# Fixed items of an expert layer: tokens found by products on TensorE in place of a scatter and a read-back through memory

## The chip, the cores and the metric

The kernel runs on one NeuronCore of a Trainium2 chip. The metric is the device time of one execution in microseconds (us). PE is TensorE (products and transposes), with PEld its weight loads; DVE is VectorE, ACT ScalarE, POOL GpSimd, SP SyncE. Matrices of weights and tokens lie in HBM, working tiles in SBUF, results of PE in PSUM.

## The reference

Three layers in a row, in fp32. (1) Attention over 2 batches, 8 heads, 576 places of 64 numbers, with rotated q and k. (2) A dense layer on the 1152 tokens: `g = h * sigmoid(1.702 h)` of `h = x @ w_in`, then `g @ w_out`, 512 to 2048 to 512. (3) A layer of eight experts, of which each token uses one:

```python
logits = x @ w_gate                      # (1152, 8)
expert_idx = np.argmax(logits, axis=1)
gate_w = softmax(logits)[token, expert_idx]
for i in range(N):                       # in order of tokens
    e = expert_idx[i]
    if counts[e] < capacity:             # 288
        disp[e, counts[e]] = x[i]; pos[i] = counts[e]; counts[e] += 1; keep[i] = True
h = np.maximum(einsum('ecd,edf->ecf', disp, w1), 0.0)
y = einsum('ecf,efd->ecd', h, w2)
out[i] = gate_w[i] * y[expert_idx[i], pos[i]]   # rows that are not kept stay 0
```

## The kernel before, in words

**Attention** (`Attention`, to L650) goes through 8 pairs of heads; an explicit table of times sets the order of its instructions. It writes its result transposed and split into a high and a low part (`xt`), because products are made of three parts each: high by high, high by low, low by high.

**The dense layer** (`Experts.first`, L904) takes the tokens in three cuts, 0 to 511, 512 to 767 and 768 to 1151. Each cut runs over the 16 slices f of the 2048 hidden numbers (`ffn`, L859): slice f of the weights is cut into high and low (`halves`, L829, `hl`: ACT copies, DVE subtracts), PE makes the hidden products `h` (L853), ACT and DVE apply the function and cut its result into `gh` and `gl` (L893 to L895), and two slices later PE adds the products into `y` (L883). At the end of a cut `y` holds one tile of 128 tokens per bank; each is copied into `row` and sent to HBM as `x2` (L935). For the first two cuts the 8 logits of a token are eight DVE instructions per tile (L943, `dot`); for the last cut (three tiles) PE transposes the rows (L967) and multiplies them by the gate weights (L976).

**Routing** (`route`, L979) runs once per batch, when the last tile with tokens of the batch has its logits: batch 0 during the third cut, batch 1 behind it. DVE finds the expert of each token, PE counts the tokens ahead of it with products of bf16 matrices of zeros and ones (`rank`, L1020 and L1023), and DVE works out `lin`, the number of the token's slot in a list (L1045 to L1054). Then POOL scatters, tile by tile, an entry of four numbers per token (row, row in the output, gate) into the list `slots` in HBM (L1069, five instructions per batch), reads the list back per item (`gather`, L1136, `ent`), and gathers the rows of `x2` that it names (L1146, `got`).

**Items.** An item is one expert with up to 288 tokens. Four items are fixed, two per batch: 3 blocks of 96 tokens, 2 of 112, 3 of 96 and 1 of 96 (`STATIC`, L35). Before an item starts, `turn` (L1157) transposes its gathered rows on PE (`tg`, L1164) into `xt`. `second` (L1205) runs `ffn` over 8 slices of the expert's weights, transposes the result back (`tr`, L1218), scales by the gate on DVE (L1221) and scatters the rows to the output (L1193). The fourth item is made by `few` (L1224). Items 2 and 3 belong to batch 1; the transposes of item 2 stand behind the last step of item 1's loop (hook 0 at L1331). A loop for surplus items (L1334) runs only when an expert has more tokens than the fixed items hold; otherwise a branch skips it.

**What sets the order.** Each engine runs its own instructions strictly in the order in which a scheduler wrote them, and waits on semaphores for the others. The scheduler ranks instructions of the whole program, so a change in routing also moves weight cuts and products that it does not touch. The loads of the weights stand on SP's queue; SP reads an item's expert from `etab` (L1296) before it loads that item's weights.

## Time and profile before

| | |
|---|---|
| median of 3 runs | 440.02 us (439.24 to 440.18) |
| the profiled execution's own time | 437.69 us |
| its span, first to last instruction | 436.0 us |
| PE busy | 423.7 us (97%) |
| DVE, ACT, POOL busy | 326.0, 264.7, 137.2 us |
| granted clock of PE | 0.998 of 2.4 GHz |

The profile is one execution. An engine's timeline lists its instructions in order of start; neighbours of one kind are drawn together (x4), the second number is the time from the first start to the last end, and a bracket behind the row says how long the engine sat idle before it and what released it. Since PE works as a pipeline, the pitch of its products is read from the start of one row to the start of the next, not from a row's length.

### The profile page before, as it was taken

The page shows a single profiled execution, that of the slowest core. Times are in us where ns is not written, and L with a number is a line of the kernel's source. Part 1 is how long each engine was busy: PE and PEld are TensorE (multiplying, and loading weights), DVE is VectorE, ACT ScalarE, POOL GpSimd, SP SyncE. Part 2 cuts the span into 40 slices and gives each one's busy share as a digit, 9 for nine tenths or more (in the row PEclk, how much of TensorE's full clock was granted, in tenths as well). Part 3 has the DMA queues.
Part 4 walks back from the last instruction along what each step waited for, and adds up shares of the span by engine and source line. Part 5 has one row for each costly group of instructions (what it writes and reads, how often), then busy time and mean ns, then how long its engine had stood idle before and what let it go on. Part 6 is the DMA issues. An engine that isn't in the chain of part 4 may idle for free.

```text
span 436.0 us, 8504 instructions
## 1 busy us (share of the span) xinstructions
PE 423.7 (97%) x3150; PEld 349.5 (80%) x3150; DVE 326.0 (75%) x762; ACT 264.7 (61%) x556; POOL 137.2 (31%) x129
## 2 busy tenths in 40 slices
PE   7899999999999999999999999999999999999994
PEld 3566766666675888888899999898898999999992
DVE  5666766678998989997379988979546489766663
ACT  1798989988777334444456565574446356563662
POOL 1988778693347200000000000007330006531012
PEclk9999999999999999999999999999999999999999
DMA  8624413711343566665015000100824447686501
GB/s 269 234 114 153 152 47 107 250 30 50 98 161 114 194 214 213 238 234 208 2 72 208 34 3 0 50 0 1 291 76 135 154 144 181 199 273 221 213 21 53
DMA packets 20686, 58.96 MB, mean 135 GB/s; under 512 B 3542, under 2 KB 5910, under 8 KB 20641
## 3 DMA queue, kind: packets, MB, share of 16 engines
q1 hardware_dynamic: 18016, 53.98, 36.9%
q0 software_dynamic: 1664, 3.62, 2.8%
q10 hardware_dynamic: 960, 0.79, 0.5%
q8 instruction: 26, 0.43, 0.4%
q14 instruction: 20, 0.16, 0.1%
HBM read 51.79 MB, written 6.67 MB: 134 GB/s over the span
## 4 chain that ended last, share of the span: by engine, by line
PE 73%; issue 12%; DVE 4%; DMA 4%; POOL 3%; ACT 1%; SPq 0%; POOLq 0%; DVEq 0%; ACTq 0%
PE y L883 23%; PE h L853 23%; PE t L601 8%; PE s L488 7%; PE t L528 7%; PE s L477 2%; PE s L747 2%; POOL out L1193 2%; DMA turns<-in_turns 1%; DMA slots<-entry,r_at 1%; DMA wf<-in_w 1%; DVE pp L500 1%; POOL got L1146 1%; POOL slots L1069 1%; DVE hl L834 1%
## 5 line engine op out<-in xcount | busy, mean ns | idle before, releaser
L853 PE MATMUL h<-xt,hl 128*128 128x256 f32 (+4 forms) x828 | 145.7, 317 | 0.0
L853 PEld LDWEIGHTS h<-xt,hl 128*128 128x128 f32 x828 | 127.2, 189 | 9.9
L834 DVE TENSOR_TENSOR hl<-wf,hl 128x1024 fp32r<-128x1024 f32 x69 | 84.5, 1225 | 28.2 <-ACT hl L833 26.8
L833 ACT ACTIVATE hl<-wf 128x1024 fp32r<-128x1024 f32 x69 | 73.2, 1060 | 37.4 <-PE y L883 21.9
L883 PE MATMUL y<-hl,gh 128*128 128x512 f32 x288 | 82.6, 392 | 0.0
L1069 POOL DMA_INDIRECT slots<-entry,r_at x10 | 16.6, 1658 | 186.1 <-DVE r_ends L992 183.7
L883 PEld LDWEIGHTS y<-hl,gh 128*128 128x128 f32 x288 | 53.1, 188 | 9.6
L500 DVE TENSOR_SCALAR_CACHE_REDUCE pp<-s 128x576 f32<-128x576 f32 x64 | 46.0, 755 | 18.9 <-PE s L488 18.5
L893 ACT ACTIVATE g<-h 128x256 f32<-128x256 f32 (+2 forms) x45 | 21.8, 484 | 57.8 <-PE h L853 55.6
L512 ACT ACTIVATE pp<-pp,nm 128x576 f32<-128x576 f32 x64 | 49.2, 774 | 11.2 <-DVE pp L500 11.1
L461 POOL TENSOR_TENSOR qk<-qk,turns 128x640 f32<-128x640 f32 (+1 forms) x30 | 44.9, 1514 | 20.2 <-DMA qk<-in_qk 20.2
L883 PE MATMUL y<-hl,gl 128*128 128x512 f32 x144 | 49.7, 391 | 0.0
L488 PE MATMUL s<-qk 64*128 64x288 f32 x256 | 40.4, 421 | 1.3 <-DVE qk L463 0.7
L601 PE MATMUL t<-pt,vr 128*64 128x288 f32 x256 | 38.0, 417 | 0.0
L895 DVE TENSOR_TENSOR gl<-g,gh 128x512 fp32r<-128x512 f32 (+2 forms) x48 | 26.6, 559 | 13.1 <-ACT gh L894 12.6
L528 PEld LDWEIGHTS t<-ident,pp 64*128 64x128 f32 x576 | 25.8, 138 | 13.1 <-issue 4.2
L943 DVE SCALAR_TENSOR_TENSOR dot<-row,dots 128x512 f32<-128x512 f32 x48 | 32.9, 685 | 1.8 <-ACT row L931 1.4
L883 PE MATMUL y<-gh,hl 128*128 128x288 f32 (+1 forms) x192 | 33.4, 289 | 0.0
L407 ACT ACTIVATE pt<-t 128x512 f32<-128x512 f32 (+1 forms) x55 | 28.5, 542 | 6.7 <-PE t L528 6.4
L528 PE MATMUL t<-ident,pp 64*128 64x64 f32 x576 | 29.8, 228 | 1.6 <-ACT ptr L407 1.1
L883 PEld LDWEIGHTS y<-hl,gl 128*128 128x128 f32 x144 | 26.4, 188 | 4.3
L488 PEld LDWEIGHTS s<-qk 64*128 64x128 f32 x256 | 24.1, 188 | 6.1 <-DVE pp L500 1.6
(189 smaller groups left out, 583.7 us busy)
## 6 DMA issues: line engine op xcount, KB each, us to landing
wf<-in_w SPq DMA_DIRECT2D x32, 512.0 KB, 5.3
qk<-in_qk SPq DMA_DIRECT2D x14, 640.0 KB, 7.2
raw<-in_w_in SPq DMA_DIRECT2D x16, 512.0 KB, 4.4
raw<-in_w_out SPq DMA_DIRECT2D x16, 512.0 KB, 3.3
vr<-in_v SPq DMA_DIRECT2D x8, 320.0 KB, 4.9
out<-got SPq DMA_DIRECT2D x9, 256.0 KB, 3.7
dots<-in_w_dots SPq DMA_DIRECT2D x4, 512.0 KB, 4.5
x<-row SPq DMA_DIRECT2D x8, 256.0 KB, 3.4
```

Source lines behind the costliest of these rows:

```text
L407: return e.activation(out=out, in_=x, func=AF.Copy)
L461: e.tensor_tensor(out=u, in0=u, in1=self.turns[:, k, ts], op=ALU.mult)
L488: nc.tensor.matmul(both[h][:, n, 0:HALF], q[hs, at:at + P], k[hs, key:key + HALF], start=True, stop=True)
L500: self.nc.vector.tensor_scalar(out=self.room(p, i).rearrange("p (n k) -> p n k", n=2), in0=self.open.pop(("s", p, i))[:, :, 0:HALF], scala ...
L512: self.nc.scalar.activation(out=x, in_=x, func=AF.Exp, scale=-1.0, bias=self.nm[p % 2][:, i:i + 1], accum_out=self.sum[p % 2][:, i, 0:1],)
L528: self.nc.tensor.transpose(banks[b][:, at:at + 64], x[bs], self.ident[bs, bs])
L601: self.nc.tensor.matmul(o[h * 64:h * 64 + 64], x, y, start=j < 2, stop=j > 7)
L833: ins = nc.scalar.activation(out=hl[:, 0], in_=t, func=AF.Copy)
L834: self.last = nc.vector.tensor_tensor(out=hl[:, 1], in0=t, in1=hl[:, 0].bitcast(F32), op=ALU.subtract).ins
L853: ins = self.nc.tensor.matmul(h, u, v, start=m == 0, stop=m == len(ops) - 1)
L883: nc.tensor.matmul(y[j][:, 0:DM if rows else w], u, v, start=f == LAG and m == 0, stop=f == n + LAG - 1 and m == 2,)
L943: ins = nc.vector.scalar_tensor_tensor(out=self.weights.m2.tile([P, DM], F32, tag="m", name="dot"), in0=row, scalar=1.0, in1=self.dots[e], ...
```

## The change

In words: (1) `lin` is no longer only an address. `mark` compares the numbers 0 to 511 (`seats`, loaded once) with each token's slot number: five DVE instructions per batch give matrices of zeros and ones, 128 tokens by 512 (batch 0) or 384 (batch 1) seats, in bf16. (2) `find` multiplies them on PE by a table with six columns per token (two digits of its number, a constant, and the gate in three bf16 parts): `who`, five products for each block of 96 or 112 seats, so 25 for batch 0 and 20 for batch 1. DVE adds the parts up and writes the entry of each seat into `found`. (3) The row gathers read `found`. Scatter and read-back of the list remain only in the branch for surplus items. (4) `find(1)` stands in the loop of item 0, `find(0)` right behind `route(0)`. (5) Of the last cut's three tiles only two are transposed and multiplied on PE; the third gets eight `dot` instructions on DVE. (6) The gate is worked out earlier in `route`.

```diff
@@ -800,9 +808,13 @@
 
         load(self.rows, d["rows"])
         load(self.masks, d["masks"])
+        load(self.seats, d["seats"])
         before = self.three.tile([P, DM], F32, name="got", bufs=4)[:, 0:P]
         load(before, d["before"])
         nc.vector.tensor_copy(out=self.before, in_=before)
+        digits = self.three.tile([P, DM], F32, name="got", bufs=4)[:, 0:3 * B * NC]
+        load(digits, d["digits"])
+        nc.vector.tensor_copy(out=self.digits[:, :, :, 0:3], in_=digits.rearrange("p (b k c) -> p b k c", b=B, c=3))
         load(self.small, d["small"])
         load(self.gate, d["w_gate"])
         pad = self.three.tile([P, DM], F32, name="got", bufs=4)[0:TT, 0:NSLOT // TT * 4].bitcast(I32)
...
@@ -925,7 +937,7 @@
         work = []
         for n, (k, t) in enumerate(zip(range(k0 // P, k1 // P), y)):
             row = self.three.tile([P, DM], F32, name="row")
-            if last and n % 2:
+            if last and n == 1:
                 nc.vector.tensor_copy(out=row, in_=t)
             else:
                 nc.scalar.activation(out=row, in_=t, func=AF.Copy)
...
@@ -935,10 +947,8 @@
                     nc.sync.dma_start(out=self.x2[b][lo - b * S:hi - b * S, :], in_=row[lo - k * P:hi - k * P])
             work.append((row, [self.logits[b][:, k - b * (NC - 1)] for b in range(B) if 0 <= k - b * (NC - 1) < NC]))
         if last:
-            self.turned_logits(work)
-            known(k1 // P - 1)
-            return
-        for k, (row, out) in zip(range(k0 // P, k1 // P), work):
+            self.turned_logits(work[:-1])
+        for k, (row, out) in list(zip(range(k0 // P, k1 // P), work))[-1 if last else 0:]:
             for e in range(E):
                 ins = nc.vector.scalar_tensor_tensor(
                     out=self.weights.m2.tile([P, DM], F32, tag="m", name="dot"),
...
@@ -949,8 +959,9 @@
                     op1=ALU.mult,
                     accum_out=out[0][:, e:e + 1],
                 )
-                if self.placed:
-                    self.tc.add_manual_dep(ins.ins, self.placed, Weights.order, reason="order")
+                before = self.low if last else self.placed
+                if before:
+                    self.tc.add_manual_dep(ins.ins, before, Weights.order, reason="order")
             for x in out[1:]:
                 nc.vector.tensor_copy(out=x, in_=out[0])
             known(k)
...
@@ -1052,31 +1069,16 @@
         tt(lin, lin, s2, ALU.add)
-        at = new("at", NC, dt=I32)
-        placed = v.tensor_copy(out=at, in_=lin)
+        placed = self.mark(b, lin, gate)
         self.placed = placed.ins.name
...
-        done = []
-        for j in range(NC):
-            ins = nc.gpsimd.indirect_dma_start(
-                out=self.slots,
...
+        self.tokens.append((at, entry))
+        if b == 0:
+            self.find(b)
...
@@ -1133,6 +1135,85 @@
+    def mark(self, b, lin, gate):
+
+        v, digits = self.nc.vector, self.digits[:, b]
+        rest = self.one.tile([P, NC], F32, name="r_rest")
+        v.tensor_copy(out=digits[:, :, 3], in_=gate)
+        v.tensor_tensor(out=rest, in0=gate, in1=digits[:, :, 3], op=ALU.subtract)
+        v.tensor_copy(out=digits[:, :, 4], in_=rest)
+        v.tensor_tensor(out=digits[:, :, 5], in0=rest, in1=digits[:, :, 4], op=ALU.subtract)
+        n = sum(math.prod(STATIC[i]) for i in (2 * b, 2 * b + 1))
+        room = self.two.tile([P, ND, HALF], F32, name="yt", bufs=1).rearrange("p j c -> p (j c)").bitcast(BF16)
+        last = self.one.tile([P, SEATS], BF16, name="taken")
+        self.taken = []
+        for k in range(NC):
+            x = (room[:, k * SEATS:(k + 1) * SEATS] if k < NC - 1 else last)[:, 0:n]
+            ins = v.tensor_scalar(
+                out=x, in0=self.seats[:, 0:n], scalar1=lin[:, k:k + 1], scalar2=-2.0 * b * HALF,
+                op0=ALU.subtract, op1=ALU.is_equal,
+            )
+            self.taken.append(x)
+        return ins
+
+    def find(self, b):
+
+        v, digits = self.nc.vector, self.digits[:, b]
+        groups = [(2, 3)] if b else [(0,), (1,)]
+        seat, column = 0, 0
+        t = self.ps_m.tile([P, 512], F32, tag="m", name="who")
+        for items in groups:
+            size = STATIC[items[0]][1]
+            blocks = sum(STATIC[i][0] for i in items)
+            u = t[0:size, column:column + 6 * blocks].rearrange("p (i c) -> p i c", c=6)
+            for i in range(blocks):
+                for k in range(NC):
+                    x = self.taken[k][:, seat:seat + size]
+                    self.nc.tensor.matmul(u[:, i], x, digits[:, k], start=k == 0, stop=k == NC - 1)
+                seat += size
+            column += 6 * blocks
+            total = self.one.tile([P, 4, 2], F32, name=f"total{items[0]}")[0:size, 0:blocks]
+            v.tensor_reduce(out=total, in_=u.rearrange("p i (a c) -> p i a c", c=3), axis=AX.X, op=ALU.add)
+            ents = self.one.tile([P, 4, 4], I32, name=f"found{items[0]}")[0:size, 0:blocks]
+            for c, far in (0, FAR), (2, FAR + b * S):
+                v.tensor_scalar(out=ents[:, :, c], in0=total[:, :, 0], scalar1=float(far), scalar2=None, op0=ALU.add)
+            v.tensor_copy(out=ents[:, :, 3].bitcast(F32), in_=total[:, :, 1])
+            at = 0
+            for item in items:
+                ent, rows = ents[:, at:at + STATIC[item][0]], []
+                at += STATIC[item][0]
+                for i in range(ent.shape[1]):
+                    row = self.three.tile([P, DM], F32, name="got", bufs=4)[0:size]
+                    self.fetch(row, b, ent[:, i, 0:1])
+                    rows.append(row)
+                self.found[item] = ent, rows
+
...
@@ -1328,17 +1402,22 @@
                 self.clear()
 
         for i in range(3):
-            self.second(found[i][0], x[i], self.expert(i, sp), ((4, 0, 4)[i], lambda: turn(i + 1)))
+            hooks = {(4, TURN, 4)[i]: lambda: turn(i + 1)}
+            if i == 0:
+                hooks[FIND] = lambda: self.find(1)
+            self.second(found[i][0], x[i], self.expert(i, sp), hooks)
         self.few(found[3][0], x[3], self.expert(3, sp))
         n = nc.values_load(self.etab[0:1, ITEMS:ITEMS + 1], min_val=4, max_val=ITEMS)
-        with tc.If(n > 4, label="more"), tc.For_i(4, n, 1, iteration_sync="staggered") as i:
-            ent, rows = self.gather(i, [0, 1])
-            tc.stage_boundary()
-            self.cut = []
-            x = self.turn(rows, 0)
-            tc.stage_boundary()
-            self.second(ent, x, self.expert(i, sp))
-            tc.stage_boundary()
+        with tc.If(n > 4, label="more"):
+            self.scatter()
+            with tc.For_i(4, n, 1, iteration_sync="staggered") as i:
+                ent, rows = self.gather(i, [0, 1])
+                tc.stage_boundary()
+                self.cut = []
+                x = self.turn(rows, 0)
+                tc.stage_boundary()
+                self.second(ent, x, self.expert(i, sp))
+                tc.stage_boundary()
 
 
 def whole(ctx, tc, d):
```

How the change moves instructions is shown at three places. `hl0_74` and `hl1_75`, or `hl_74` and `hl_75`, are the two halves of the ring of cut weights.

PE at the end of the third cut, before and then after (`tr<-ident,row` transposes a tile, `tr<-gate` makes its logits, `h 128x288` belongs to item 0):

```order
L853 MATMUL h<-xt,hl_74 128x288 x2
L967 MATMUL tr<-ident,row 128x128 x4
L853 MATMUL h<-xt,hl_74 128x288 x22
L967 MATMUL tr<-ident,row 128x128 x8
L976 MATMUL tr<-gate,yt 128x8 x4
L883 MATMUL y_3921<-gh,hl_74 128x288 x2
L853 MATMUL h<-xt,hl_75 128x288 x12
L976 MATMUL tr<-gate,yt 128x8 x4
L976 MATMUL tr<-gate,got 128x8 x4
```

```order
L865 MATMUL h<-xt,hl_74 128x288 x2
L978 MATMUL tr<-ident,row 128x128 x4
L865 MATMUL h<-xt,hl_74 128x288 x22
L978 MATMUL tr<-ident,row 128x128 x4
L987 MATMUL tr<-gate,yt 128x8 x4
L895 MATMUL y_3941<-gh,hl_74 128x288 x2
L895 MATMUL y_3942<-gh,hl_74 128x288 x2
L895 MATMUL y_3943<-gh,hl_74 128x288 x2
L865 MATMUL h<-xt,hl_75 128x288 x12
L987 MATMUL tr<-gate,yt 128x8 x4
```

One tile's four transposes and its four products with the gate weights are gone.

DVE where the slot numbers of batch 1 become final, before and then after (`yt` and `taken` hold the matrices of `mark`):

```order
L992 TENSOR_TENSOR r_lin<-r_lin,r_s_3807 128x5
L834 TENSOR_TENSOR hl_75<-wf,hl_75 128x1024
L992 TENSOR_TENSOR r_lin<-r_lin,r_s_3808 128x5
L1056 CAST r_at<-r_lin 128x5
L992 TENSOR_TENSOR r_ends<-r_base,r_items 128x8
```

```order
L1003 TENSOR_TENSOR r_lin<-r_lin,r_s_3859 128x5
L846 TENSOR_TENSOR hl_74<-wf,hl_74 128x1024
L1003 TENSOR_TENSOR r_lin<-r_lin,r_s_3860 128x5
L1152 TENSOR_SCALAR yt<-seats,r_lin 128x384 x4
L1152 TENSOR_SCALAR taken<-seats,r_lin 128x384
L1075 CAST r_where_3880<-r_lin 128x5
L1003 TENSOR_TENSOR r_ends<-r_base,r_items 128x8
```

The five comparisons stand right behind the final slot numbers, and the cut of weights ahead of them is one slice further on (the other half of the ring).

PE where item 0 ends and item 1 (`128x224`) begins, before and then the start of the new products of batch 1:

```order
L883 MATMUL y3_3924<-gh_4134,hl1_75 128x288 x2
L883 MATMUL y3_3924<-gl_4135,hl1_75 128x288
L853 MATMUL h_4260<-xt_59,hl0_74 128x224 x12
L883 MATMUL y0_3921<-gh_4163,hl1_75 128x288 x2
L883 MATMUL y1_3922<-gh_4163,hl1_75 128x288 x2
```

```order
L895 MATMUL y3_3944<-gh_4197,hl1_75 128x288 x2
L895 MATMUL y3_3944<-gl_4198,hl1_75 128x288
L865 MATMUL h_4323<-xt_59,hl0_74 128x224 x6
L895 MATMUL y0_3941<-gh_4226,hl1_75 128x288 x2
L1172 LDWEIGHTS yt_3873
L1172 MATMUL who_4108<-digits_1876,yt_3873 96x6
L895 MATMUL y1_3942<-gh_4226,hl1_75 128x288 x2
```

Four of the first five `who` stand between products of the layers, one by one; the other sixteen follow each other.

## Rows read from the trace of the kernel before

**Rows 1.** Timeline by windows, all engines: busy us and instructions, granted clock, DMA share, GB/s.

```profile
core 0: us, PE busy (x) PEld busy (x) DVE busy (x) ACT busy (x) POOL busy (x), PEclk, DMA share, GB/s
336.00:346.00 10.00, 10.00 (x83) 9.80 (x82) 5.63 (x13) 4.81 (x9) 0.00 (x0) 1.00 0.56 204
350.00:360.00 10.00, 10.00 (x79) 10.00 (x78) 9.22 (x32) 4.91 (x8) 0.00 (x0) 1.00 0.49 157
360.00:370.00 10.00, 10.00 (x84) 10.00 (x82) 9.11 (x37) 6.56 (x12) 6.74 (x5) 1.00 0.75 172
410.00:420.00 10.00, 10.00 (x81) 10.00 (x80) 5.76 (x11) 6.56 (x15) 0.00 (x0) 1.00 0.38 144
```

**Rows 2.** Timeline of PE, last tile of tokens: start us, us, line, operation.

```profile
336.26 0.66 PE L967 MATMUL tr<-ident,row 128*128 128x128 f32 x4
336.67 3.14 PE L853 MATMUL h<-xt,hl 128*128 128x288 f32 x22
339.65 1.03 PE L967 MATMUL tr<-ident,row 128*128 128x128 f32 x8
...
344.07 1.04 PE L976 MATMUL tr<-gate,got 128*128 128x8 f32 x8
344.97 0.38 PE L883 MATMUL y<-gl,hl 128*128 128x288 f32 x1
```

**Rows 3.** Timeline of PE, rank products of batch 1 and transposes behind them.

```profile
349.53 0.20 PE L1020 MATMUL rank<-r_oh,before 128*128 128x48 bf16 x1
349.57 0.27 PE L1023 MATMUL rank<-r_oh,ones 128*128 128x40 bf16 x5
349.70 0.58 PE L1164 MATMUL tg<-ident,got 112*128 112x112 f32 x4
350.05 0.51 PE L883 MATMUL y<-gh,hl 128*128 128x288 f32 x2
```

**Rows 4.** Source lines 1020, 967, 1218, weight loads: ns min/median/max, first and last start.

```profile
L1020 PEld LDWEIGHTS <-before x2: 96/96/97, 290.2 to 349.5; 128*128 128x128 bf16 x2
...
L967 PEld LDWEIGHTS tr<-ident,row x12: 138/140/143, 336.3 to 340.3; 128*128 128x128 f32 x12
...
L1218 PEld LDWEIGHTS tr<-ident,yt x32: 124/127/134, 368.9 to 425.8; 128*96 128x96 f32 x24, 128*112 128x112 f32 x8
```

**Rows 5.** Source line 703 and groups by line, DVE (busy us, mean ns, idle before).

```profile
L703 DVE TENSOR_SCALAR m<-raw x32: 388/422/1035, 102.3 to 201.0; 128x512 uint32<-128x512 uint32 x32
...
L943 DVE SCALAR_TENSOR_TENSOR dot<-row,dots 128x512 f32<-128x512 f32 x48 | 32.9, 685 | 1.8 <-ACT row L931 1.4
...
L834 DVE TENSOR_TENSOR hl<-wf,hl 128x1024 fp32r<-128x1024 f32 x69 | 84.5, 1225 | 28.2 <-ACT hl L833 26.8 <-issue 1.0
```

**Rows 6.** Timeline of DVE, the seat number of batch 1 is final.

```profile
359.51 0.16 DVE L992 TENSOR_TENSOR r_lin<-r_lin,r_s 128x5 f32<-128x5 f32 x1
```

**Rows 7.** Timeline of PE where items read what routing found.

```profile
299.70 1.92 PE L853 MATMUL h<-xt,hl 128*128 128x384 f32 x10
...
364.75 1.49 PE L853 MATMUL h<-xt,hl 128*128 128x224 f32 x12
...
379.90 0.49 PE L1164 MATMUL tg<-ident,got 96*128 96x96 f32 x4
...
390.11 2.81 PE L853 MATMUL h<-xt,hl 128*128 128x288 f32 x20
```

**Rows 8.** Timeline of POOL, batch 1: first scatter, first row gather.

```profile
360.16 1.01 POOL L1069 DMA_INDIRECT slots<-entry,r_at  x1 [31.90 <-DVE r_ends L992]
...
375.76 1.04 POOL L1146 DMA_INDIRECT got<-x,ent  x1 [1.82 <-PE h L853]
```

**Rows 9.** Source line 1296, SP reads an item's expert: count, ns, first and last start.

```profile
L1296 SPq TENSOR_LOAD <-etab x4: 267/286/466, 303.2 to 366.1; - x4
```

**Rows 10.** Timeline of all engines, the end.

```profile
430.17 0.68 ACT L1292 ACTIVATE row<-y,ent 96x512 f32<-96x512 f32 x1 [2.17 <-PE y L1282]
431.13 0.92 POOL L1193 DMA_INDIRECT out<-row,ent  x1 [1.70 <-ACT row L1292]
```

More of the change, by code (lines that the diff above doesn't have):

```diff
@@ L36 @@
 ROWS = 20
+SEATS = 512
+FIND = 3
+TURN = 0
 NSLOT = ITEMS * HALF
@@ L775, in prepare @@
         self.oh = one.tile([P, NC + 1, E], BF16, name="r_oh")
+        self.seats = one.tile([P, SEATS], F32, name="seats")
+        self.digits = one.tile([P, B, NC, 6], BF16, name="digits")
         self.small = one.tile([P, NC * E + 2 * ROWS * E + ROWS], F32, name="small")
@@ L1209, in second @@
         w = blocks * size
-        y = self.ffn(x, [lambda f=f: self.slice_of(expert, f) for f in range(F2 // P)], self.relu, {hook[0]: hook[1]} if hook else {})
+        y = self.ffn(x, [lambda f=f: self.slice_of(expert, f) for f in range(F2 // P)], self.relu, hooks)
         yt = self.two.tile([P, ND, HALF], F32, name="yt", bufs=1)
@@ L1310, in run @@
         found, x = {}, {}
+        self.found, self.tokens = found, []
         def turn(i):
```

68 lines of the change are left out of this document (40 added, 28 removed).

## The prediction, made before the changed kernel ran

> **What bounds the kernel now.** I read the table of waits first, which names no wait of PE in the stretch of the change, and then the timeline by windows, because a busy PE can still be one that crawls. In the four windows of [rows 1] PE is busy for all of the 10 us; the reader is to see that the counts fit as well: the last window holds 81 products, 123 ns each, and 22 products of 288 columns fill the time from 336.67 to the next transposes at 339.65, some 135 ns each with the changes of kind [rows 2]. There is no hole that a shorter wait could close. The clock is granted in full (1.00 in these windows). So from the dense layer to the end the time is the sum of what PE has to do, and behind the last product come only ACT's copy, POOL's last scatter and its landing [rows 10], which the change leaves alone.
>
> The chain that the change shortens is not a bound. In batch 1 the first scatter starts at 360.16 and the first row gather is issued at 375.76 [rows 8]; the first transpose that needs a gathered row starts at 379.90, and item 2, which reads it, at 390.11 [rows 7]. That is 15.6 us from slot numbers to gather, and PE meanwhile is filled with item 0 and item 1. The gain to be had from removing it is nothing, unless something else moves.
>
> **What goes from PE.** Of the third tile four transposes and its four products with the gate weights disappear. Four transposes take from 336.26 to 336.67, 0.41 us; one tile's gate products from 344.07 to 344.97, 0.90 us [rows 2]. Since PE is the bound and nothing fills the hole except PE's next work, all of it counts: -1.31 us.
>
> **What comes to PE.** 45 products `who`: 15 with 96 seats and 10 with 112 for batch 0, 20 with 96 for batch 1. Each moves only six columns, so its price is that of loading its weights. The trace of before has no bf16 load of that width, so I bound it. Below: the rank products of the same type, six of them from 349.53 to 349.70, 28 ns each [rows 3], give 45 x 0.028 = 1.3 us. Above: the fp32 transposes right behind, four from 349.70 to 350.05, 88 ns each [rows 3], give 3.9 us. Between them I use the loads themselves [rows 4]: a transpose's load of 128 columns takes 140 ns, one of 96 columns 124 to 127 ns, so a column costs about 0.45 ns; 35 loads of 96 and 10 of 112 columns are 35 x 0.043 + 10 x 0.050 = 2.0 us. I take 2.0 us, because the operand is narrower than 128 columns like these, and bf16 should not be dearer than a transpose in one pass. Nine of the 45 stand one by one between wide products, where a load can hide; I leave that in the bound below.
>
> The 128-column bf16 load of the rank products takes 96 ns and lets the next one start after 28 [rows 3, 4]. The Trainium skill, on the page "TensorE: Matmul & The Clock Gate", section "Weight-path perf modes", says that the fast weight load is used when the number of weights is 128 and the type isn't FP32; the trace agrees as far as it goes, and by this rule blocks of 96 and 112 would not get it. By the page's formula in the section "LDWEIGHTS", columns divided by 1.2, an estimate for the 45 loads is 3.7 us, and the sum would be +2.4 us.
>
> **DVE.** It gains ten comparisons (`mark`), eight steps for the gate's parts, eight small ones in `find` and eight `dot`, and loses one copy of a turned tile. A two-step comparison with a scalar on 512 numbers is nearest to the line that cuts integers, 0.42 us median [rows 5]: 5 x 0.42 = 2.1 us for batch 0, and for batch 1 with 384 numbers 1.6 us, if the cost goes by length. Eight `dot` are 8 x 0.685 = 5.5 us [rows 5], in a stretch, 336 to 346, in which DVE is now busy for 5.63 of 10 us [rows 1]. Small steps are 0.16 us long [rows 6] and start every 0.1. So the route of batch 1 begins about 0.8 us later. All this lies beside PE, as long as it stays ahead of it; of DVE's own time nothing is on the path.
>
> **Where PE now waits for DVE.** `who` waits for the comparisons, and on PE everything stands behind `who`. Batch 0: the slot numbers are final near 295.7, five comparisons end near 298.5, and the first `who` comes after four of the ten products that start at 299.70 [rows 7], near 300.4. Two us are in hand. Batch 1 is tighter: DVE is over 91% busy from 350 to 370 [rows 1], final slot numbers are written at 359.51 [rows 6], and the order now puts one more cut of weights (1.2 us, [rows 5]) and some smaller steps ahead of them; with the later start I get 361.9, and the end of the comparisons at 363.5. The first `who` of batch 1 stands behind six of the products that start at 364.75 [rows 7] and two more; with what goes and comes ahead of it that is near 365.1. It leaves 1.6 us, so I cost the wait at nothing; if the comparisons cost 0.685 us each, like a `dot`, it is 0.1 to 0.3 us, and more if the weight cuts wait for ACT.
>
> **What is moved past queues.** POOL loses ten scatters and the loads of the lists, and keeps its row gathers and output scatters in the same order; from 350 to 360 it has no work at all, and 6.74 us of it in the next ten [rows 1], so nothing is gained or lost. Item 2's rows are asked for some 6 us earlier, which only lengthens a wait in a buffer. On SP two loads move ahead of the read of item 2's expert, which DVE writes later by about the comparisons and `find`, 3 us; before it is read at 366.1 [rows 9], and item 2 starts at 390.11 [rows 7]: covered by 20 us. The two loads in the setup (`seats`, `digits`) and a small cast fall where DVE cuts weights ahead of PE; the cast is shorter than 0.42 us [rows 5], and costs that much at most if the cuts are no longer ahead. The surplus branch is skipped before and after: by the inputs no expert has tokens left over that the fixed items don't take, so the scatter in it doesn't run.
>
> **The sum.** -1.31 + 2.0 = +0.7 us, between 0.0 and +2.6 by the bounds of the loads. Against the profiled execution's own 437.69 us that is 438.4. That execution lies 2.33 us under the median of the runs; the same step on the median, 440.02, gives **440.7 us**. It is +0.16%, less than the 0.2% (0.88 us) that a measurement of this kernel can tell from no change.
>
> **Rivals.**
>
> *Slow loads.* The 45 loads run at the pitch of the fp32 ones, 88 ns: 3.9 - 1.31 = +2.6 us, 442.6. For it: width below 128. Against: two bytes a number instead of four. The page's rule above leads here. Chance 0.18.
>
> *PE stalls behind the comparisons.* DVE, over 91% full in these 20 us, finishes the comparisons of batch 1 after 365.1 instead of at 363.5. From there each us late is a us of PE. Three us later than I reckon, from comparisons at a `dot`'s price (+1.1) and two weight cuts waiting for ACT at this place, is a stall of 1.4; with the loads at 2.0 it makes +2.1 us, 442.1. For it: the order leaves no other work in `who`'s place. Against: 1.6 us in hand. Chance 0.13.
>
> *Cheap loads.* They cost what the rank products cost: 1.3 - 1.31 = 0, 440.0, no change. For it: same type, same back-to-back place for 36 of them. Chance 0.19.
>
> *A gain.* The loads are cheap, nine hide fully (36 x 0.028 = 1.0), and PE's new order saves the small losses at changes between kinds of products, for which I allow 0.7 us by the difference between 135 ns and the 123 ns of [rows 1] over some sixty products: 1.0 - 1.31 - 0.7 = -1.0 us, 439.0. Against: nothing in the change aims at it. Chance 0.12.
>
> **How the numbers follow.** My forecast (loads at the width's price, no stall) has 0.38. Of it, loads dearer than 48 ns pass the 0.88 us, which I put at 0.09, and 0.03 falls on the faster side by other shifts of the order. Faster: 0.12 + 0.03 = 0.15. Slower: 0.18 + 0.13 + 0.09 = 0.40. Same: the forecast's remaining 0.26 and 0.19 of the cheap loads, 0.45. The range goes from 439.2, where most of the gain case is left out, to 443.0, which takes in the slow loads and the stall; the forecast alone would be 439.9 to 441.5.
>
> **What would show it.** In the changed profile: the pitch from `who` to `who` in the two rows of 11 and 16 that stand together (43 ns if right, 28 or 88 in the rivals); no PE idle time released by `yt` or `taken`, and the comparisons near 0.4 us; PE busy in every window from 230 us on; the first row gather of batch 1 some 6 us ahead of 375.76 with item 2 no earlier for it. I am wrong if PE has idle time before `who`, if item 2's transposes come earlier and the end with them, or if the end moves by more than PE's own products do.

## The result, and the profile after

| | before | changed |
|---|---|---|
| median of 6 runs each | 439.14 us (438.08 to 440.18) | 442.50 us (442.00 to 443.27) |
| ratio | | 1.0079, 95% interval 1.0057 to 1.0101 |
| profiled execution, span | 437.69, 436.0 us | 442.13, 440.4 us |
| start of PE's last product | 429.73 us | 432.91 us |
| start of POOL's last scatter to the end of the span | 4.87 us | 6.09 us |
| DVE, POOL busy | 326.0, 137.2 us | 336.0, 118.4 us |

The change made the kernel slower, by 3.4 us of the medians. The forecast was 440.7 us, +0.7 us: the measured time lies inside the range given, and outside the forecast's own 439.9 to 441.5. The two profiled executions lie 4.4 us apart, because that of before was 1.45 us under the median of these six runs and that of after 0.37 us. In some executions the granted clock averages 0.98 to 0.99 instead of 0.996 or more, and most of these are 2 to 4 us longer; the medians contain such executions, and the ratios leave out those that are over 1.5% above the fastest of their kernel.

First the windows in which the forecast argued, and one more, of the kernel after (columns as in [rows 1]):

```profile
336.00:346.00 10.00, 10.00 (x75) 9.45 (x74) 8.89 (x20) 4.95 (x10) 0.00 (x0) 1.00 0.68 236
350.00:360.00 10.00, 10.00 (x84) 9.93 (x83) 8.72 (x25) 6.03 (x9) 0.00 (x0) 1.00 0.55 177
360.00:370.00 10.00, 10.00 (x92) 9.97 (x91) 9.21 (x36) 5.35 (x10) 0.00 (x0) 1.00 0.42 141
370.00:380.00 10.00, 9.16 (x81) 8.88 (x80) 6.73 (x23) 3.48 (x7) 6.03 (x6) 1.00 0.71 218
```

PE is full up to 370, as before; DVE went from 5.63 to 8.89 us in the first window and POOL from 6.74 to nothing in the third. What is new is the last line: PE lacks 0.84 us between 370 and 380, some twelve microseconds behind the place where the forecast had looked for a wait, ahead of `who`.

The timeline of PE after, at the last tile, the products `who` and the hole (start us, us, line, operation; a bracket is idle time and its releaser):

```profile
338.09 0.66 PE L978 MATMUL tr<-ident,row 128*128 128x128 f32 x4
...
341.49 0.60 PE L978 MATMUL tr<-ident,row 128*128 128x128 f32 x4
341.93 0.96 PE L987 MATMUL tr<-gate,yt 128*128 128x8 f32 x8
...
345.20 0.95 PE L987 MATMUL tr<-gate,yt 128*128 128x8 f32 x8
...
299.92 0.86 PE L865 MATMUL h<-xt,hl 128*128 128x384 f32 x4
300.62 0.17 PE L1172 MATMUL who<-digits,yt 128*96 128x6 bf16 x1
300.65 0.42 PE L865 MATMUL h<-xt,hl 128*128 128x384 f32 x1
300.91 0.17 PE L1172 MATMUL who<-digits,yt 128*96 128x6 bf16 x1
...
301.77 0.17 PE L1172 MATMUL who<-digits,taken 128*96 128x6 bf16 x1
...
302.24 0.95 PE L865 MATMUL h<-xt,hl 128*128 128x384 f32 x4
...
366.21 0.17 PE L1172 MATMUL who<-digits,yt 128*96 128x6 bf16 x1
...
367.54 0.17 PE L1172 MATMUL who<-digits,taken 128*96 128x6 bf16 x1
...
368.24 0.77 PE L895 MATMUL y<-gl,hl 128*128 128x288 f32 x4
...
377.57 0.39 PE L895 MATMUL y<-gh,hl 128*128 128x224 f32 x2
378.79 0.48 PE L865 MATMUL h<-xt,hl 128*128 128x224 f32 x2 [0.84 <-issue]
```

Last tile: two groups of four transposes stand where three stood, and eight of 24 gate products are gone (the trace has two records for each product of the program) [rows 2]. `who`: from the start of the eleven at 301.77 to 302.24 is 43 ns each; the sixteen from 367.54 to 368.24 take 44 ns each; the row of ten with 112 seats took 49. Eight stand alone: four wide products take 0.70 us, 175 ns each, ahead of 300.62, but from one lone `who` to the next, with one wide product between, it is 0.29 us (300.62 to 300.91), so a lone one costs 0.11 us. The hole: two products of 0.11 us each start at 377.57, and the next starts at 378.79, 1.0 us late. The bracket says "issue": the profile shows no engine that PE waited for.

What ACT, POOL and DVE did around the hole, in the same kernel, one timeline each. ACT:

```profile
376.23 0.36 ACT L911 ACTIVATE gh<-h 128x224 fp32r<-128x224 f32 x1 [4.83 <-remote]
377.69 1.06 ACT L845 ACTIVATE hl<-wf 128x1024 fp32r<-128x1024 f32 x1 [1.09 <-PE h L865]
```

POOL:

```profile
370.50 1.03 POOL L1192 DMA_INDIRECT got<-x,found  x1 [40.16 <-DVE etab L1099]
371.83 1.19 POOL L1192 DMA_INDIRECT got<-x,found  x1 [0.30 <-PE tr L1293]
373.32 0.97 POOL L1192 DMA_INDIRECT got<-x,found  x1 [0.30 <-issue]
374.59 0.96 POOL L1192 DMA_INDIRECT got<-x,found  x1 [0.30 <-issue]
375.86 0.95 POOL L1268 DMA_INDIRECT out<-row,found  x1 [0.30 <-issue]
377.11 0.94 POOL L1268 DMA_INDIRECT out<-row,found  x1 [0.30 <-issue]
...
434.31 0.92 POOL L1268 DMA_INDIRECT out<-row,found  x1 [1.70 <-ACT row L1367]
```

DVE, the end of the route of batch 1:

```profile
362.97 0.16 DVE L1003 TENSOR_TENSOR r_lin<-r_lin,r_s 128x5 f32<-128x5 f32 x1
363.16 1.41 DVE L1152 TENSOR_SCALAR yt<-seats,r_lin 128x384 bf16<-128x384 f32 x4
364.48 0.42 DVE L1152 TENSOR_SCALAR taken<-seats,r_lin 128x384 bf16<-128x384 f32 x1
```

The comparisons end at 364.9 and the first `who` of batch 1 starts at 366.21, without a wait. The first row gather goes out at 370.50, 5.3 us ahead of before [rows 8]. ACT's copy `gh` at 376.23 reads a product of the group that ran from 372.58 to 374.18: the copy starts 2.0 us later, with "remote" as releaser, the profile's word for one that it can't place. The trace also keeps the moments at which each engine's counter moves, on which the other engines wait: PE's counter moves at 371.79 and next at 376.21, though the product that moves it ended at 374.17 by the profile. So what came late is PE's signal, and ACT answered it at once. The next weight cut on ACT waits for PE's next signal and ends at 378.75, and PE's next product, which reads it, starts at 378.79. Over these 8 us POOL issues six indirect transfers 1.25 to 1.5 us apart without a pause. At the end, from POOL's last scatter at 434.31 to the span's end at 440.4 are 6.09 us, against 431.13 to 436.0 before [rows 10].

What POOL does there, by source line: L1411 is the branch around the loop for surplus items, L1449 the end of the program (kernel after), and L1370 the end of the program in the kernel before (count, ns min/median/max, first and last start us):

```profile
L1411 POOLq EVENT_SEMAPHORE  x4: 17/43/1652, 435.6 to 435.8; - x4
L1411 POOLq INC_SWDGE_SEM  x1: 539/539/539, 437.5 to 437.5; - x1
...
L1449 POOLq DRAIN  x3: 45/107/1527, 438.1 to 440.2; - x3
```

```profile
L1370 POOLq DRAIN  x3: 46/103/3123, 432.1 to 435.7; - x3
```

Before, one drain of 3.12 us starts at 432.1, 0.9 us behind the last scatter, and covers its landing. After, POOL first waits on its queues' counters at the skipped branch, 1.65 us for the last of them, which is that of the last scatter; then comes an instruction of 0.54 us that adds to a counter of its queues, and only then the drain, 1.53 us. The kernel before has nothing of POOL's at its branch but the branch itself.

### The profile page after: what moved, and what is told of

It is laid out like the page before. It is cut to its first block, busy times and chain, and to the rows that moved or that the text cites. A ratio compares the mean times of both kernels' runs of the same rounds, so it can differ in the third digit from the quotient of the medians.

```text
span 440.4 us, 8583 instructions
## 1 busy us (share of the span) xinstructions
PE 424.9 (96%) x3183; PEld 350.6 (80%) x3183; DVE 336.0 (76%) x808; ACT 264.4 (60%) x556; POOL 118.4 (27%) x115
## 4 chain that ended last, share of the span: by engine, by line
PE 75%; issue 12%; POOL 4%; DVE 3%; DMA 2%; ACT 2%; another core or an unknown queue 1%; POOLq 0%; DVEq 0%
PE y L895 25%; PE h L865 24%; PE t L607 8%; PE s L494 6%; PE t L534 6%; PE s L753 2%; PE s L483 2%; POOL qk L467 2%; POOL out L1268 1%; DMA qk<-in_qk 1%; DMA turns<-in_turns 1%; POOL qk L469 1%; DVE pp L506 1%; PE tg L1238 0%
## 5 line engine op out<-in xcount | busy, mean ns | idle before, releaser
L895 PE MATMUL y<-hl,gh 128*128 128x512 f32 x288 | 83.7, 391 | 0.0
L1192 POOL DMA_INDIRECT got<-x,found x9 | 11.1, 1236 | 219.8 <-DVE found L1180 160.5
L895 PE MATMUL y<-hl,gl 128*128 128x512 f32 x144 | 50.7, 392 | 0.0
L953 DVE SCALAR_TENSOR_TENSOR dot<-row,dots 128x512 f32<-128x512 f32 x56 | 38.4, 685 | 1.7 <-ACT row L943 1.2
```

Source lines behind the costliest of these rows:

```text
L895: nc.tensor.matmul(y[j][:, 0:DM if rows else w], u, v, start=f == LAG and m == 0, stop=f == n + LAG - 1 and m == 2,)
L953: ins = nc.vector.scalar_tensor_tensor(out=self.weights.m2.tile([P, DM], F32, tag="m", name="dot"), in0=row, scalar=1.0, in1=self.dots[e], ...
```

## The experiments

Each was timed beside runs of the kernel before on the same chip; the ratio is to these.

**1. Is it the tile's logits or the search?** The first kernel is the one before with only the last tile's logits moved to DVE (the diff's parts in `first` and `turned_logits`):

```diff
+            self.turned_logits(work[:-1])
+        for k, (row, out) in list(zip(range(k0 // P, k1 // P), work))[-1 if last else 0:]:
```

> The kernel before, with the last tile's logits by eight products on VectorE and nothing else of the change. Theory (PE has no hole, so its own work is the time): four transposes and four gate products go, -1.3 us against before, 437.8; no idle time of PE behind 230 us; from POOL's last scatter to the end of the span 4.8 us as before. Rival (the eight products, 5.5 us of DVE, make the route of batch 1 late, and PE waits for item 2's rows): 0 to +2 us against before, with idle time of PE near 380.

Measured: 443.18 us against 438.45, ratio 1.0046 (1.0011 to 1.0081), the runs spread from 437.83 to 447.06. The rival's wait is there in the one execution of which there is a trace. Of POOL, then PE:

```profile
365.47 1.01 POOL L1068 DMA_INDIRECT slots<-entry,r_at  x1 [33.52 <-DVE r_ends L991]
...
381.25 1.03 POOL L1145 DMA_INDIRECT got<-x,ent  x1 [2.51 <-DMA ent<-slots]
```

```profile
385.34 0.52 PE L1163 MATMUL tg<-ident,got 96*128 96x96 f32 x4 [2.27 <-DMA got<-x,ent]
```

This execution was late from the start: the rank products of batch 0 stand at 293.94 instead of 290.24, behind a granted clock of 0.73 from 10 to 20 us. Less these 3.7 us the first scatter comes 1.6 us later than before and the first gather 1.8 us later [rows 8]; that was enough for PE to wait 2.27 us for the rows. Behind the wait the granted clock averages 0.83 from 380 to 390 us, and by 391 PE has lost another 1.7 us. So in this execution the distance that the scatter and read-back of before keep to PE was used up by the dots. It is not shown for the kernel: four of the twelve executions took 437.83 to 440.34 us, on both sides of before. Where it holds, the dots need the search, and the forecast costed each part by itself.

The second kernel is the changed one with the third tile back on PE:

```diff
-            self.turned_logits(work[:-1])
+            self.turned_logits(work)
```

> The changed kernel with the third tile's logits back on PE. Theory: +1.3 us against the changed kernel, 443.8, that is +4.7 against before: 45 products with their places 2.7, a stall of PE of 1.0 near 378 us, the end 1.2 later. Rival (the products on VectorE make DVE late and so cause the stall near 378): the stall goes, +0.3 against the changed kernel, 442.8.

Measured: 441.92 us (441.49 to 442.40), ratio 1.0060 (1.0040 to 1.0079); last product at 432.55, from the last scatter to the end 6.16 us. Giving 1.31 us back to PE made the kernel no slower than the change: this one has no hole near 378 (PE 10.00 of 10 us from 370 to 380).

**2. The end.** The changed kernel without the ten scatters in the branch that is skipped. With these inputs the outputs don't need them.

```diff
         with tc.If(n > 4, label="more"):
-            self.scatter()
```

> The changed kernel without the ten scatters in the branch for surplus items (left out: surplus items would find no list; these inputs have none, the branch is skipped). In the changed kernel 6.1 us lie between the start of POOL's last scatter and the end of the span, 4.8 before; POOL has waits and an increment of its queue's semaphores there that before has not. Theory (the skipped branch must do the bookkeeping of the scatters that didn't run, behind the last landing): 4.8 to 5.0 us again, -1.2 us, 441.3. Rival (the last scatter of that execution only landed later): no change, 442.5.

Measured: 439.66 us (439.25 to 442.68), ratio 1.0028 (1.0004 to 1.0051). ACT's copy, POOL, and PE's last product:

```profile
373.90 0.36 ACT L911 ACTIVATE gh<-h 128x224 fp32r<-128x224 f32 x1 [2.81 <-PE h L865]
```

```profile
374.27 0.96 POOL L1192 DMA_INDIRECT got<-x,found  x1 [0.31 <-issue]
375.54 1.95 POOL L1268 DMA_INDIRECT out<-row,found  x1 [0.30 <-DVE r_z L1003]
377.79 0.94 POOL L1268 DMA_INDIRECT out<-row,found  x1 [0.30 <-DVE gl L912]
...
432.83 0.92 POOL L1268 DMA_INDIRECT out<-row,found  x1 [1.70 <-ACT row L1367]
```

```profile
431.43 0.40 PE L1357 MATMUL y<-hl,gl 128*96 128x512 f32 x1
```

The last scatter at 432.83 is 4.77 us ahead of the end at 437.6: code that is never run cost 1.3 us, all of it behind the last scatter, and POOL goes from the branch straight to a drain (2.65 us) again. Over before the median is 1.2 us, where the change has 3.4: more is gone than the end. The rest is the hole, which isn't there, though the instructions up to the end are the same. POOL's four gathers go out at the pitch of the change (370.17, 371.49, 373.00, 374.27), and ACT's copy at 373.90 is on time; that POOL's issue at 375.54 then took 1.95 us instead of 0.95 can't have helped it.

**3. The loads of `who`.** 128 seats are loaded where 96 or 112 are needed, and all 512 seats are compared for both batches:

```diff
-                    x = self.taken[k][:, seat:seat + size]
+                    x = self.taken[k][:, seat:seat + span]    # span = min(P, SEATS - seat)
```

> The changed kernel with the products who loaded with 128 seats each instead of 96 or 112 (the last block of batch 0 stays at 112; the rows beyond a block are not read) and all 512 seats compared in both batches. Theory (a bf16 load of 128 columns is faster than one of 96): load 96 ns instead of 125, pitch 28 instead of 43 and 48 ns in the rows of 10 and 11, about -0.6 us for the 36 that stand together, 441.9. Rival (pitch goes by columns): 58 ns, +0.6 us, 443.1. Second rival (another part of the product sets the pitch): 43 ns, no change.

Measured: 441.76 us (440.88 to 444.16), ratio 1.0066 (1.0041 to 1.0091). PE:

```profile
301.37 0.18 PE L1174 MATMUL who<-digits,yt 128*128 128x6 bf16 x1
301.41 0.42 PE L865 MATMUL h<-xt,hl 128*128 128x384 f32 x1
301.67 0.18 PE L1174 MATMUL who<-digits,yt 128*128 128x6 bf16 x1
...
302.02 0.24 PE L1174 MATMUL who<-digits,yt 128*128 128x6 bf16 x4
...
302.27 0.95 PE L865 MATMUL h<-xt,hl 128*128 128x384 f32 x4
...
372.95 0.65 PE L1295 MATMUL tr<-ident,yt 128*96 128x128 f32 x4 [0.51 <-DVE row L1298]
```

In a row the wide load goes at 25 ns (ten from 302.02 to 302.27) instead of 43. A lone one costs as much as before, 0.12 us (301.37 to 301.67 less 175 ns). Of the gain, 0.5 us went into a new wait for DVE, which has 512 seats to compare in place of 384.

**4. Chance or change?** The changed kernel once more, on another chip than the first three experiments, to see whether the hole near 378 belongs to one execution:

> The changed kernel once more, as the control of this set. In its first profile PE stood still for 1.0 us near 378, because ACT copied two slices of item 1's hidden numbers and weights some 2 us after PE had put them out; the run without the scatters in the branch, whose instructions are the same up to the end, had no such hole. Theory A (the hole is chance, not order): no hole near 378 in this profile, last product of PE at 431.4 to 432.0. Theory B (the hole belongs to the changed order): 1 us again, last product at 432.9. Either way 6.1 us from POOL's last scatter to the end.

Measured: 442.52 us (441.56 to 443.66), ratio 1.0072 (1.0045 to 1.0099). ACT again sat idle for 4.78 us before its copy, by "remote", until 377.90, 2.0 us behind the end of the products, and PE lost about 0.25 and 0.6 us at 379 and 380. So the hole is not one execution's. It is not the change's alone either: the second, third and fourth kernel keep POOL's transfers as they are and have none.

**5. Other orders.** Two kernels meant to save the lone products or the scatters. In the first, `who` begins its sum with the matrix that is written last, so that all its products stand in rows:

```diff
-                for k in range(NC):
+                for k in reversed(range(NC)):
```

> The changed kernel with each sum of five products who begun with the matrix that VectorE writes last, so that the four or five that stood one by one between wide products now stand with the others. In the changed kernel a product that stands alone between two wide ones moves the next by 0.10 to 0.11 us, one in a row 0.043 to 0.049. Theory (a lone product costs its whole load and more): nine lone ones become members of a row, 9 x 0.065 = -0.6 us, 441.9 if the changed kernel is at 442.5. Rival (lone ones hide behind wide products, as my bound below assumed): +0.2 us, since nine more cost a full pitch.

Measured: 444.19 us (442.46 to 445.24), ratio 1.0114 (1.0085 to 1.0143). A miss: the lone products were gone, but the order behind them shifted too, and PE waited for DVE's `row` (0.52 us at 372.82) and, by the profile, for a small step of the route (1.13 us at 374.59). The second scatters and reads back for batch 0, as the kernel before, searches for batch 1 alone, and has no scatter in the branch:

```diff
+        if b == 0:
+            placed = v.tensor_copy(out=at, in_=lin)
+        else:
+            placed = self.mark(b, lin, gate)
```

> What the runs so far say would pay: batch 0 as before (scatter, read-back), batch 1's tokens found by products with 128 seats per load, all twenty in one row, its scatter ahead of the row gathers outside the branch, and the last tile's logits on VectorE. Theory (PE's own work and the end): -1.31 for the last tile, 20 x 0.025 + 0.2 at the two seams = +0.7, the end as before: -0.6 us against before, 437.8 with before at 438.4; the first row gather of batch 1 near 370, no idle time of PE from 230 on. Rival (VectorE, with eight products more, is late for who or for the weights of item 1, as the first changed profile and the run with the products alone show): holes of 0.5 to 2 us between 366 and 390, +0 to +1.5 us against before.

Measured: 445.29 us (443.96 to 449.62), ratio 1.0159 (1.0117 to 1.0201); PE was busy for 6.15 of the 10 us from 370 to 380. Here POOL has five scatters of batch 1 just ahead of its gathers. The same without the reversed sums:

> The hybrid (batch 0 by scatter and read-back, batch 1 by products with 128 seats, scatters outside the branch, last tile's logits on VectorE), with each sum begun with the matrix that is written first, so that four of the products stand alone as in the changed kernel. In the hybrid with all twenty in one row PE stood still for 3.3 us in four holes between 375 and 380 for weights of item 1, and 2 us near 369 for item 0's result. Theory A (the row of twenty, waiting for the last comparison, shifted the work of VectorE behind it): the holes go, 0.3 to 0.6 us under before, 437.9 to 438.2. Theory B (the scatters of batch 1 on POOL ahead of the row gathers, and the read of the lists, hold things up): holes as in the first hybrid, 444 to 445.

Measured: 445.10 us (444.60 to 448.39), ratio 1.0152 (1.0105 to 1.0199). ACT, then the window:

```profile
380.23 0.36 ACT L911 ACTIVATE gh<-h 128x224 fp32r<-128x224 f32 x1 [9.72 <-remote]
```

```profile
370.00:380.00 10.00, 6.87 (x47) 5.23 (x45) 4.30 (x12) 0.51 (x3) 6.76 (x7) 1.00 0.69 197
```

With eleven indirect transfers in a row instead of six ACT stands still for 9.7 us, and the hole grows to 3.1 us; PE's counter does not move from 372.99 to 380.21. This kernel has half of the comparisons, so they are not needed for the hole. On the same chip the kernel of experiment 6, with seven transfers in a row, loses about 1.5 us: there the hole is larger with more of them.

**6. The end mended.** Scatters inside the loop over surplus items, with the wide loads of the third experiment:

```diff
         with tc.If(n > 4, label="more"):
-            self.scatter()
             with tc.For_i(4, n, 1, iteration_sync="staggered") as i:
+                self.scatter()
```

> The changed kernel with two mends: the ten scatters stand in the loop for surplus items instead of the branch around it, and who loads 128 seats at a time. Theory: from POOL's last scatter to the end 4.8 us again (-1.3), 36 products in rows at 25 ns instead of 43 and 48 (-0.7): -2.0 us against the changed kernel, 440.5, if VectorE is not late for item 0's result (in the run with 128 seats PE waited 0.7 us for it near 372, because five comparisons of 512 seats take 0.15 to 0.3 us more); then -1.3, 441.2. Rival (the end depends on the scatters being in the program at all): -0.7 us, 441.8.

Measured: 445.32 us (441.62 to 447.35), ratio 1.0146 (1.0104 to 1.0187); the traced execution is the fastest of six that spread over 5.7 us, so only its trace is read. From the last scatter to the end it is 4.73 us: the end is mended with the scatters still in the program. But the hole is there, larger (about 0.5 and 1.0 us from 378.5 to 380), and with it no gain.

**7. The hole.** Two kernels change POOL's transfers alone, on a chip on which the changed kernel itself was not run. In one, POOL writes zeros into an unused tile behind each row gather of batch 1, a pause of 0.55 us:

```diff
+                        idle = self.one.tile([P, 512], F32, name="idle")
+                        rest = nc.gpsimd.memset(idle, 0.0)
```

> The changed kernel with a memset of 0.7 us on POOL behind each of batch 1's four row gathers, which changes nothing else. In all six profiles with holes in PE near 370 to 380 POOL's four gathers and the scatters behind them start 1.25 to 1.35 us apart without a longer one, and in these 8 us ACT starts its copies 1 to 10 us after the product they read; in the three profiles of the change's variants without holes, one or more of POOL's took 1.4 to 1.9 us. Theory (signals of PE and ACT are held up while POOL issues gathers back to back with the weights' loads): with a pause in between the hole near 378 goes, -0.7 to -1.0 us against the changed kernel, 441.6. Rival (the hole has nothing to do with POOL): the hole stays, 442.5, or grows as item 0's scatters come 3 us later.

Measured: 441.63 us (440.75 to 444.38), ratio 1.0079 (1.0051 to 1.0108). The profiled execution has no hole (PE 10.00 of 10 us from 370 to 380), and ACT's copies start within 0.3 us of the end of their products. Over before it costs 3.0 us by the medians, where the change costs 3.4. In the other the row gathers of batch 1 are plain loads of fixed rows; the rows that `found` names are not fetched:

```diff
+                    if b:
+                        ins = self.nc.scalar.dma_start(out=row, in_=self.x2[b][i * size:(i + 1) * size])
```

> The changed kernel with batch 1's four row gathers replaced by plain loads of fixed rows on ACT's queue behind found (left out: the rows named by found are not fetched, so batch 1's results are those of other tokens). The same bytes move; POOL issues nothing between 369 and item 0's scatters. Theory (POOL's row of gathers holds up the signals): no hole near 378, ACT's copies start within 0.3 us of the product they read, -0.7 to -1.0 us against the changed kernel, 441.6. Rival (the traffic itself, rows and weights together, holds them up): the hole stays, 442.5.

Measured: 441.68 us (441.00 to 442.30), ratio 1.0062 (1.0045 to 1.0080). Again 3.0 us over before, and no hole, though the DMA share from 370 to 380 is 0.84, more than with it.

These two don't settle the cause, because the chip changed with the kernel. Kernels that were built together ran on one chip, later ones on another, and the traces differ by these sets. In six traces, those of experiments 1, 2, 3 and 7 from two chips, no move of PE's counter comes more than 0.15 us behind the end of its product in the whole execution, with pauses or without, with scatters in a row or not. In the other eight, those of before, of the change and of experiments 4, 5, 6 and 8, some come late, at worst by 1.2 us (before) to 6.6 us (the kernel with eleven transfers). All but one of these 57 late moves fall to products that end while POOL runs a transfer or at most 0.6 us behind one. So rows of transfers go with the late signals, but they don't suffice for them, and on the chip of this experiment there may have been no hole to remove. The test that is missing is the changed kernel and the one with pauses on one chip on which signals come late.

**8. All repairs together**, in a kernel that leaves nothing out, on one more chip: pauses, scatters inside the loop, and 128-seat loads only where the compared seats reach (no longer comparisons).

> All repairs in one kernel that leaves nothing out: the scatters stand inside the loop over surplus items, POOL pauses behind each row gather of batch 1, and each sum of who loads up to 128 seats of the compared ones (15 blocks-by-tiles of 20 get 128 columns per batch's number of seats; the comparisons keep their length). Theory (the terms are the end 1.25, the hole about 1.0, and the pitch of the loads in rows, some 30 x 0.02 = 0.6): 442.5 - 2.8 = 439.7 us, ratio about 1.002 to the kernel before; tail near 4.8 us, no hole near 378, no wait for DVE beyond that of the kernel as changed. Rival (the terms overlap, or the order shifts and another wait comes, as in the kernel with the wide loads and the one with the reversed sums): 441 us or more, with PE idle time before the transposes of item 1.

Measured: 439.88 us (439.22 to 442.36) against 438.94, ratio 1.0015 (0.9989 to 1.0040). The windows, then POOL, then ACT:

```profile
370.00:380.00 10.00, 10.00 (x92) 9.95 (x91) 7.50 (x23) 3.28 (x7) 8.75 (x11) 1.00 0.83 254
```

```profile
373.32 0.97 POOL L1202 DMA_INDIRECT got<-x,found  x1 [0.16 <-issue]
374.29 0.54 POOL L1196 MEMSET idle<- 128x512 f32 x1
374.99 0.97 POOL L1202 DMA_INDIRECT got<-x,found  x1 [0.16 <-issue]
...
432.71 0.92 POOL L1278 DMA_INDIRECT out<-row,found  x1 [1.69 <-ACT row L1377]
```

```profile
379.23 1.06 ACT L845 ACTIVATE hl<-wf 128x1024 fp32r<-128x1024 f32 x1 [2.54 <-PE y L895]
```

PE is full, the end takes 4.8 us again (432.71 to 437.5), and over before 0.9 us are left by the medians of the 3.4. But the pauses did not keep the signals on time: ACT's cut at 379.23 waited for a product that ended at 377.01, 2.2 us earlier. That PE lost nothing by it is shown for this execution; which of the repairs kept it full is not. Of PE's own products -1.31 us and some 2.2 for `who` would leave those 0.9 us (the rows of 11, 10 and 16 now take 0.29, 0.40 and 0.52 us, the lone ones about 1.0); in the traces PE's last product starts 1.6 us behind that of before, so the agreement is not close. No kernel of this study beat the one before; this one can't be told from it.

## Why the prediction was right or wrong

**The account.** Terms of the 3.4 us, each with where it was measured in the two traces:

| term | forecast | measured | from |
|---|---|---|---|
| last tile's products leave PE | -1.31 | -1.3 | the timeline of PE: four transposes and a third of the gate products gone |
| 45 `who` on PE | +2.0 | +2.5 | 11, 10 and 16 in rows 0.47 + 0.49 + 0.70; eight alone 0.9 |
| PE waits in batch 1 | 0 | +1.0 | the hole at 378; absent in six kernels |
| the end | 0 | +1.2 | 6.09 against 4.87 us; gone without the scatters in the branch |
| sum | +0.7 | +3.4 | the medians differ by 3.36, the two traces by 4.4 |

That the sum meets the medians is in part luck. The traces from which it is read differ by 4.4 us. Of the 1.0 us between, 0.25 is the later start, and most of the rest stands around `who`: in the third kernel of the study, without a hole, PE's last product starts at 431.43, 1.7 us behind before, and with the 1.3 us that left this gives 3.0 for `who` with its places; what in these places costs the 0.5 us is open. On the other side 34 executions of the kernel before, in the first experiments, have a median of 438.45 us, where the six here have 439.14.

**The bound** was right: PE is full but for the hole, and the shorter chain of batch 1 (rows gathered 5.3 us earlier, forecast 6) brought nothing; item 2's products start at 393.22, later than at 390.11 [rows 7].

**The last tile** was right to the row.

**`who`, the term of the sum that was mis-sized.** In rows the estimate of 43 and 50 ns from the fp32 loads was right to a nanosecond or two, and by luck in part: it took only what a load grows by with each column and left out, without a reason, the larger part of the 124 to 127 ns that a load of 96 columns takes [rows 4]. The step that failed is "where a load can hide": the ones between wide products cost 0.11 us each, more than twice those in a row, and being wide on 128 columns did not help them. The rival of slow loads at 88 ns and that of cheap ones at 28 ns both fell. The Trainium skill, "TensorE: Matmul & The Clock Gate", section "Weight-path perf modes", gives the fast load to 128 weights that aren't FP32: the runs agree (median load 125 ns, pitch 43 at 96 columns; load 96 ns, pitch 25 at 128). The estimate of 3.7 us from the same page's load formula came out too high: in a row the pitch counts, 43 ns, and not the duration, 125.

**DVE.** The forecast had the last slot numbers at 361.9 (measured 362.97), the comparisons ended at 363.5 (364.9) and the first `who` near 365.1 (366.21). Each came about a microsecond late, of which 0.25 us is this execution's later start (rank products of batch 0 at 290.49 instead of 290.24), and 1.3 us stayed in hand where 1.6 were reckoned; a comparison took 0.42 to 0.49 us, not the 0.69 of a `dot`. The rival of a stall behind the comparisons fell in the changed kernel.

**The step that failed most** stands under "What is moved past queues": POOL "keeps its row gathers and output scatters in the same order ... so nothing is gained or lost". The order is the same, but they moved: six indirect transfers now go out in a row from 370.5 on, and while they do, PE's signals come up to 2.0 us late, and PE loses 1.0 us where the forecast had nothing. The place and the price are shown, in both traces of the changed kernel. The cause stays open. In eight traces signals come late around rows of POOL's transfers, in that of the kernel before too (PE's by up to 1.2 us, without a loss of PE); in the six from two chips they don't, with the same row of gathers. Through what they are held, and why the sets differ, no view shows. Pauses are not shown to help. Nor is a longer issue of POOL's what lets the signals through: in the third and fourth kernel ACT's copies at 373.90 and 375.17 were on time before POOL's first issue of over 1.5 us (375.54 and 377.16).

**The other step that failed** is "the scatter in it doesn't run", costed at nothing, and with it that the change leaves the end alone. The scatter doesn't run, and still the end became 1.2 us longer. The rows of L1411 show by what: at the skipped branch POOL waits until its last scatter has landed, adds to a counter of its queues, and only then starts the drain that before ran during the landing. All seven kernels with scatters directly in the branch have this increment, of 0.46 to 0.54 us; the seven without have none, and taking the scatters out, or putting them a level deeper into the loop, gives it all back. Of the forecast's own signs of being wrong it was this one that came true: the end moved by more than PE's own products do.

**The chances.** Slower had 0.40 and was the outcome, for neither of the two reasons that this chance was made of. That the range held the time is luck: its upper end, 443.0, took in slow loads and a stall, which did not come, and these happened to be worth what the hole and the end cost.

## What to carry to other kernels

Where PE is the bound, a chain that is shortened off its path is worth nothing, but everything that the shorter chain lets start earlier lands somewhere: look at what will stand in a row on POOL's queue then. A branch that is skipped isn't free if it issues indirect transfers; put them as deep inside as they are used, and look at the skipped branch in the trace, by its source line. When a hole comes and goes between kernels, compare them on one chip before naming its cause: here the hole went with the chip as well as with the edit. Tiny products belong in rows: alone between wide ones each costs as much as two or three.

## What the runs showed that was not expected

- In eight of fourteen traces signals come late around POOL's indirect transfers: in the change ACT's release by 2.0 us (4.83 us of idle time), with eleven transfers in a row by 6.6 us (9.72 us of idle time). In the other six, from two chips, no signal of PE's is more than 0.15 us late, with such rows too.
- Ten scatters that are never run stretched the end, from POOL's last scatter on, to 5.96 to 6.18 us in all seven kernels that have them directly in the branch; it is 4.73 and 4.79 us with them inside the loop, 4.87 before, and 4.77 to 5.19 in the four others that have none there.
- A bf16 load's pitch in a row is 25 ns at 128 columns, 43 at 96 and 49 at 112; between wide products a tiny one costs 0.11 to 0.12 us at either width.
